# Threshold attention with Fourier mixing on one core: other work held back for a mixing, and its sums on VectorE cut into three pieces

## The chip, the cores and the metric

The kernel runs on one NeuronCore of one Trainium2 chip. Its time is the device time of one launch, in microseconds. Lower is better.

## The reference

The program computes an attention with a threshold and, on its result, a mixing by Fourier transforms and a two-layer network. All data are float32.

```python
# q, k, v: (8, 8, 576, 64); tau = 0.02; w_ch1: (512, 2048); w_ch2: (2048, 512)
scores = q @ k.T / sqrt(64)
scores = where(scores >= max(scores) - tau, scores, -1e9)
attn   = softmax(scores) @ v                      # (B, H, S, D)
x      = attn.transpose(0, 2, 1, 3).reshape(B, S, H * D)   # (8, 576, 512)
mixed  = real(fft(fft(x, axis=1), axis=2))
u      = x + mixed
un     = (u - mean(u)) / sqrt(var(u) + 1e-6)      # over the last axis
out    = u + maximum(un @ w_ch1, 0) @ w_ch2
```

## The kernel before, in words

**Attention.** There are 8 batches of 8 heads. Two heads make a pair, so a batch has 4 pairs, and a pair has 5 steps of 128 query rows (`NT = 5`, the last one holds what is left of both heads). A batch is thus 20 steps (`per_batch`), and the whole program 160. Step `i` calls `scores(i)` (L424, TensorE into the PSUM tile `sc`), `softmax(i)` (L451: maxima at L462 and threshold at L478 on VectorE, the exponential at L470 on ScalarE, the division at L494 on VectorE), `weights_in_parts(i - 1)` (L511: TensorE transposes of the step before, at L540 and L559, copied to SBUF by ScalarE), and twice per pair `weighted_values` (L568).

**Mixing.** When a pair is complete, `fold_rows` (L610) adds and subtracts its rows against each other, on GpSimd for the first three pairs of a batch and on VectorE for the last (L619), into the tile `f`. Then `mixing(b)` (L660) makes the transform of batch `b`. It is a Python generator, and each `yield` ends one of its steps. Its first step holds all the sums across the chunks of `f` on VectorE: two by `fold_chunks` (L650, L651) and five at L669, L675 and L678. Two empty steps follow. The next six make matmuls `py` from `f` (L689) and copy them to `y_e` and `y_o` on ScalarE (L694, L699). The last five are matmuls `pa` (`over_seq`, L702) whose results go through the tile `tmp` (ScalarE L721, VectorE L725 and L726) and are added to the attention's result on GpSimd (L728, L732), which writes the tile `u_t`. That is 14 steps.

**Groups.** The network works on groups of tokens: one of 384, one of 128 (`channels`, L828), then sixteen of 256 tokens, numbered 2 to 17 (`channels_in_quarters`, L1035). Each of those sixteen multiplies 2x2 blocks with seven products in place of eight. Its first product, `hidden_in_quarters` (L885), is 14 pieces of 16 matmul records (L923) each; VectorE adds their PSUM banks to the tile `hs` (L932), ScalarE copies some and takes the Relu (L937), VectorE and GpSimd form the sums of weights (L906). The three pieces `first`, `others`' sixth and `others`' seventh accumulate in one PSUM bank, `banks["sum"]`: the sixth is read by VectorE (L973) before the seventh is added to the same bank (L982). Its second product is seven products of 4 pieces each (L1064, matmuls at L1066). GpSimd forms sums of `hs` (`s_form`, L1062), VectorE sums of `w2` (`combine`, L1027), and VectorE adds each result to the rows (`Rows.add`, L801); SyncE then issues the store (L808). One bank, `sum_`, is held from its first product to its sixth. All these PSUM tiles share one pool of four banks (tag `mm`) with the mixing's and with the attention's transposes.

**The planner.** TensorE's order is written out by `fill` (L1137), which is called three times in each step. Each call adds `per_slot` to a budget, takes one step of a mixing if there is one, and then takes pieces of group work while less has been spent than the budget. Group work of a batch may start once that batch's mixing is done (`work[0][0] < mixed`). The unit is a matmul's row count times four; a piece of the first product is 4096 units, a piece of the second 2048, a whole group 115712, of which the second product is 57344. A mixing is 19240 units, spread over its last 11 steps. At the end of a batch's last step, `start_batch` (L1260) queues the next mixing and the groups that it completes, and sets `per_slot` so that after 60 calls the work left over is `keep` (L1269). So while a mixing runs, TensorE fills the time with the attention and with what `keep` left of the group before. For all batches but the first, `keep` is 0.4 x 198144 = 79258 units. Batches 1 to 7 bring 2, 2, 3, 2, 2, 2 and 3 groups of 256 tokens. After step 160 there is no attention; `per_slot` is then 4953 units until everything is done. This stretch is called the drain below. In steps 20 to 39 (`second_batch`) the order on all engines is by hand; from step 40 on only TensorE's is, and the other engines' order is chosen by the compiler's scheduler, which takes ready instructions by their place in the program.

Of the kernel before, what the change touches and what calls it, by code (L numbers as in the profile page):

```python
# [12 lines left out]
ALU = mybir.AluOpType  # L13
# [5 lines left out]
def _reversed(ap):  # L19

    n = ap.shape[1]
    return bass.AP(
        tensor=ap.tensor,
        offset=ap.offset + n - 1,
        ap=[list(ap.ap[0]), [-1, n]],
    )
# [21 lines left out]
def kernel(  # L48
# [12 lines left out]
    nc = tc.nc  # L61
    B, H, S, D = q.shape
    DM = H * D
# [13 lines left out]
    GT, BT = 384, 256  # L77
    FIRST = 2
    NG = FIRST + (B * S - GT - 128) // BT
    NK = NJ // 2  # L80
# [12 lines left out]
    f = const.tile([128, ND, 2 * FW], FP32, name="f")  # L93
# [77 lines left out]
    for u in range(2):  # L171
# [10 lines left out]
        out=q_scale[:], in0=tau_t[:], scalar1=0.0, scalar2=SCALE, op0=ALU.is_ge, op1=ALU.mult  # L182
# [3 lines left out]
        out=below[:], in0=tau_t[:], scalar1=0.0, scalar2=-3.0e38, op0=ALU.is_lt, op1=ALU.mult  # L186
# [3 lines left out]
        out=tau_pos[:], in0=tau_t[:], scalar1=0.0, scalar2=-1.0, op0=ALU.max, op1=ALU.mult  # L190
# [79 lines left out]
    plus, minus, flip = (factors[:, c : c + 1] for c in range(3))  # L270
# [378 lines left out]
    def fold_chunks(eng, b, c):  # L649
        eng.tensor_tensor(out=sums[b][:, c, :], in0=f[:, c, :], in1=f[:, c + 2, :], op=ALU.add)  # L650
        eng.tensor_tensor(  # L651
            out=f[:, c + 2, :], in0=f[:, c, :], in1=f[:, c + 2, :], op=ALU.subtract
        )
# [6 lines left out]
    def mixing(b):  # L660
        x = xs.pop(b)
        slot = slice(S * (b % 2), S * (b % 2) + S)

        E, O = slice(0, FW), slice(FW, 2 * FW)
        fold_chunks(nc.vector, b, 0)
        s01 = sums.pop(b)
        nc.vector.tensor_tensor(out=f[:, 0, E], in0=s01[:, 0, E], in1=s01[:, 1, E], op=ALU.add)  # L669
        for out_, in0, factor, in1 in (  # L670
            (f[:, 1, E], s01[:, 1, E], flip, s01[:, 0, E]),
            (f[:, 2, E], f[:, 3, E], minus, f[:, 2, E]),
            (f[:, 3, O], f[:, 2, O], plus, f[:, 3, O]),
        ):
            nc.vector.scalar_tensor_tensor(  # L675
                out=out_, in0=in0, scalar=factor, in1=in1, op0=ALU.mult, op1=ALU.add
            )
        nc.vector.tensor_tensor(out=f[:, 0, O], in0=s01[:, 0, O], in1=s01[:, 1, O], op=ALU.subtract)  # L678
        for _ in range(3):
            yield 0  # L680

        COS = ((0, 0, 65), (1, 65, 129), (2, 129, 257))
        SIN = ((0, 0, 128), (3, 128, 256))
        for u, r, n in ((0, 0, 128), (1, 128, 48), (2, 176, 128)):
            for odd in range(2):
                py = ps.tile([128, 512], FP32, tag="mm", bufs=4, name="py")
                table, first = (dim_s, 0) if odd else (dim_c, 1)
                for c, c0, c1 in SIN if odd else COS:
                    nc.tensor.matmul(  # L689
                        py[0:n, c0:c1], f[:, c, odd * FW + r : odd * FW + r + n],  # L690
                        table[:, c0:c1], start=True, stop=True, skip_group_check=True,
                    )
                y = y_o if odd else y_e
                nc.scalar.copy(  # L694
                    y[0:n, u, 0:256].rearrange("p (g hi lo) -> p lo hi g", hi=2, lo=2),
                    py[0:n, first : first + 256].rearrange("p (lo hi g) -> p lo hi g", lo=2, hi=2),
                )
                if not odd:
                    nc.scalar.copy(y[0:n, u, 256:257], py[0:n, 0:1])  # L699
                yield MIX / 11  # L700

        def over_seq(y, odd, cols, m):  # L702
            pa = ps.tile([128, 512], FP32, tag="mm", bufs=4, name="pa")
            for parity, u, table, extra in ((0, 0, seq_even, seq_xe), (1, 2, seq_odd, seq_xo)):
                at = pa[0:m, parity:KH:2]
                nc.tensor.matmul(  # L706
                    at, y[:, u, cols], table[:, odd, :], start=True, stop=False,
                    skip_group_check=True,
                )
                nc.tensor.matmul(  # L710
                    at, y[:, 1, cols], extra[:, odd, :], start=False, stop=True,
                    skip_group_check=True,
                )
            return pa

        for t in range(2):
            cols = slice(128 * t, 128 * t + 128)
            tmp = sb.tile([128, 3, KH], FP32, tag="tmp", bufs=1, name="tmp")
            low, high, sin = (tmp[:, c, :] for c in range(3))
            pb = over_seq(y_o, 1, cols, 128)  # L720
            nc.scalar.copy(sin, pb[:, 0:KH])  # L721
            yield MIX / 11
            pa = over_seq(y_e, 0, cols, 128)

            nc.vector.tensor_tensor(out=low, in0=pa[:, 0:KH], in1=sin, op=ALU.subtract)  # L725
            nc.vector.tensor_tensor(out=high, in0=pa[:, 0:KH], in1=sin, op=ALU.add)  # L726
            def add(c, rows, first, second, eng=nc.gpsimd):
                eng.tensor_tensor(  # L728
                    out=u_t[rows, c, slot.start : slot.start + KH],
                    in0=x[c][rows, 0:KH], in1=first, op=ALU.add,  # L730
                )
                eng.tensor_tensor(  # L732
                    out=u_t[rows, c, slot.start + KH : slot.stop],
                    in0=x[c][rows, KH:S], in1=_reversed(second[:, 1:HALF]), op=ALU.add,
                )

            every = slice(0, 128)
            add(t, every, low, high, nc.vector if b == 0 and t == 1 else nc.gpsimd)
            add(3 - t, every, high, low)
            if t == 1:  # L740
                add(3, slice(0, 1), high[0:1, :], low[0:1, :])
            yield MIX / 11
            if t == 1:

                pa = over_seq(y_e, 0, slice(256, 257), 1)
                nc.scalar.copy(sin[0:1, :], pa[0:1, 0:KH])
                add(2, slice(0, 1), sin[0:1, :], sin[0:1, :])
                yield MIX / 11
# [4 lines left out]
    def tokens_of(g):  # L753

        if g < FIRST:
            return ((0, GT), (GT, 128))[g]
        return GT + 128 + BT * (g - FIRST), BT

    def cost(g):

        n = tokens_of(g)[1]
        both = NJ * ND * n + NJ * DM * n // 128
        return 4 * (both if g < FIRST else both * 7 // 8) + ND * n
# [64 lines left out]
    def channels(g):  # L828
        rows = Rows(g)
        n = tokens_of(g)[1]  # L830
        h = [hs[:, n * j : n * (j + 1)] for j in range(NJ)]
        for j in range(NJ):
            hidden(g, j, j, h[j])
            yield 4 * ND * n
            if j in (2, 5) and j // 3 < rows.nt:
                rows.load(j // 3)
                yield ND * 128
            if j == 11:
                rows.factors(0, min(rows.nt, 2))
        if g == FIRST - 1:  # L840
            first_sums_w1()
        for t in range(rows.nt):
            po = ps.tile([128, DM], FP32, tag="mm", bufs=4, name="po")
            for j in range(NJ):
                nc.tensor.matmul(  # L845
                    po[:, :], h[j][:, 128 * t : 128 * (t + 1)], w2[j],
                    start=(j == 0), stop=(j == NJ - 1),
                )
                if j % 2 == 1 and j < NJ - 1:
                    yield 2 * 4 * DM  # L850
            rows.add(t, slice(0, DM), po[:, :])
            rows.store(t)
            yield 2 * 4 * DM
            if t + 2 < rows.nt:
                rows.load(t + 2)
                rows.factors(t + 2, t + 3)
                yield ND * 128
# [402 lines left out]
    def start_batch(b):  # L1260

        nonlocal groups, todo, per_slot, budget
        mixes.append(mixing(b))
        todo += MIX
        while groups < NG and sum(tokens_of(groups)) <= (b + 1) * S:
            work.append((b, channels(groups) if groups < FIRST else channels_in_quarters(groups)))
            todo += cost(groups)
            groups += 1
        keep = 0.4 * cost(0) + (cost(1) if b == 0 else 0)  # L1269
        per_slot = (todo - spent - keep) / (3 * per_batch)  # L1270
        budget = spent

# [10 lines left out]
    def second_batch(i):  # L1283
# [10 lines left out]
        if first == 0:  # L1294
# [5 lines left out]
            while folds:  # L1300
                fold_more()
            load_v(n + 1)
            start_batch(0)
            mix(3)
            mix(3)
# [123 lines left out]
```

## Time and profile before

| what | value |
|---|---|
| three runs, us | 1720.28, 1721.44, 1721.71 (median 1721.44) |
| the profiled execution's own time, us | 1722.82 |
| its span, first to last instruction, us | 1721.0 |
| mean granted TensorE clock | 0.987 |
| TensorE matmul busy, us (share) | 1639.9 (95%) |
| VectorE busy, us (share) | 1187.5 (69%) |
| ScalarE busy, us (share) | 776.9 (45%) |
| GpSimd busy, us (share) | 655.1 (38%) |
| VectorE sums of the last mixing start, us | 1518.05 |

The page gives busy time, engine by engine, then the span cut into 40 slices, then the chain of work that ended last, and then groups of equal instructions. A group's line ends with the idle time its engine had just before them and with what ended it. A line of a timeline gives start, duration, engine, source line and the tiles written and read; a figure in square brackets is how long the engine had stood idle before, and the instruction after the arrow ended that wait. Two matmul records belong to one float32 matmul, and their durations overlap, so durations of a run of them are read from the merged line of the timeline and not from the mean of one. Steps, calls and leftover work are not in the profile; they follow from the planner's arithmetic above.

### The profile page before, as it was taken

What the parts mean: (1) busy time and instruction counts of PE and PEld (TensorE: products, weight loads), DVE (VectorE), ACT (ScalarE), POOL (GpSimd) and SP (SyncE); (2) the same over time, 40 slices, a digit from 0 to 9 for tenths busy, and PEclk for the clock granted to TensorE, in tenths of its full rate; (3) what the DMA queues carried; (4) which work ended last, traced back from release to release, by engine and by line L of the source; (5) the groups of instructions that cost most, each with busy time, mean ns of one, the idle gap of its engine ahead of it and who ended that gap; (6) DMA issues with size and microseconds to landing.
All of it is one profiled execution on the core that took longest, in us unless ns stands there. A gap on an engine that the chain in (4) does not pass through costs nothing.

```text
span 1721.0 us, 28994 instructions
## 1 busy us (share of the span) xinstructions
PE 1639.9 (95%) x10838; PEld 1288.7 (75%) x10838; DVE 1187.5 (69%) x2710; ACT 776.9 (45%) x1735; POOL 655.1 (38%) x827
## 2 busy tenths in 40 slices
PE   8988899999998999999999899989999899989998
PEld 4555555467787787878788778777878688889998
DVE  6885786657666777767677777777687767754555
ACT  5864675433545353535354435354545435332111
POOL 5773563041422533243451154215250344235333
PEclk9999999999999999999999999999999999999999
DMA  5323222010010001001010000101111010000000
GB/s 160 110 53 106 71 71 54 14 34 21 20 36 17 17 23 41 22 15 34 13 29 27 22 24 12 41 22 22 27 28 34 15 34 1 14 1 13 13 13 13
DMA packets 130385, 57.49 MB, mean 33 GB/s; under 512 B 121123, under 2 KB 121125, under 8 KB 130246
## 3 DMA queue, kind: packets, MB, share of 16 engines
q1 hardware_dynamic: 128854, 55.35, 11.9%
q8 instruction: 86, 1.41, 0.4%
q14 instruction: 53, 0.43, 0.1%
q10 hardware_dynamic: 1392, 0.30, 0.1%
HBM read 46.02 MB, written 9.44 MB: 32 GB/s over the span
## 4 chain that ended last, share of the span: by engine, by line
PE 77%; DVE 12%; ACT 7%; issue 2%; POOL 1%; DMA 1%; SPq 0%; DVEq 0%; ACTq 0%; POOLq 0%
PE po L1066 22%; PE ph L923 21%; PE pv L588 8%; PE sc L434 7%; PE pw L559 5%; PE po L845 3%; DVE e L478 2%; ACT e L470 2%; DVE neg L462 2%; PE sc L445 2%; PE ph L819 1%; PE py L689 1%; PE pa L706 1%; PE pd L112 1%; PE pa L710 1%
## 5 line engine op out<-in xcount | busy, mean ns | idle before, releaser
L462 DVE TENSOR_REDUCE neg<-sc 128x1 f32<-128x576 f32 x288 | 205.7, 750 | 184.2 <-PE sc L434 170.8
L470 ACT ACTIVATE e<-sc,neg 128x576 f32<-128x576 f32 x288 | 211.8, 735 | 245.4 <-DVE neg L462 244.8
L478 DVE SCALAR_TENSOR_TENSOR e<-sc,thr,e 128x576 f32<-128x576 f32 x288 | 226.9, 813 | 52.5 <-ACT thr L474 52.0
L1066 PE MATMUL po<-w,hs 128*128 128x256 f32 x1024 | 243.2, 383 | 0.2
L923 PE MATMUL ph<-u_t,w 128*128 128x128 f32 x1536 | 196.6, 284 | 28.1 <-DVE hs L932 24.4
L923 PEld LDWEIGHTS ph<-u_t,w 128*128 128x128 f32 x1536 | 186.1, 199 | 34.2 <-DVE hs L932 25.9
L1066 PEld LDWEIGHTS po<-w,hs 128*128 128x128 f32 x1024 | 186.5, 190 | 33.3 <-issue 10.8
L561 ACT COPY e_t<-pw 128x512 f32<-128x512 f32 x256 | 148.5, 594 | 88.9 <-PE pw L559 88.7
L559 PE MATMUL pw<-ident,e 128*128 128x128 f32 x1152 | 170.2, 274 | 11.4 <-ACT kT L407 2.9
L434 PE MATMUL sc<-kT,qT 64*128 64x288 f32 x1024 | 168.0, 433 | 7.8 <-DVE e L478 7.1
L932 DVE TENSOR_TENSOR hs<-ph,hs 128x512 f32<-128x512 f32 x160 | 107.2, 684 | 78.0 <-PE ph L923 60.0
L559 PEld LDWEIGHTS pw<-ident,e 128*128 128x128 f32 x1152 | 134.5, 141 | 32.0 <-issue 4.7
L434 PEld LDWEIGHTS sc<-kT,qT 64*128 64x128 f32 x1024 | 92.7, 188 | 69.4 <-issue 42.5
L801 DVE SCALAR_TENSOR_TENSOR u<-po,rstd,u 128x256 f32<-128x256 f32 (+1 forms) x164 | 75.8, 482 | 85.4 <-PE po L1066 82.5
L937 ACT ACTIVATE hs<-hs 128x512 f32<-128x512 f32 x128 | 79.8, 631 | 118.7 <-DVE hs L932 118.6
L494 DVE TENSOR_SCALAR e<-e,den 128x576 f32<-128x576 f32 x216 | 129.3, 635 | 2.8
L923 PE MATMUL ph<-t_u,s_w 128*128 128x128 f32 x1024 | 125.2, 276 | 1.1 <-ACT y_e L699 1.0
L1062 POOL TENSOR_TENSOR s_tile<-hs 128x512 f32<-128x512 f32 x32 | 45.6, 1425 | 209.3 <-ACT hs L937 154.7
L923 PEld LDWEIGHTS ph<-t_u,s_w 128*128 128x128 f32 x1024 | 119.0, 192 | 5.1 <-issue 1.9
L1066 PE MATMUL po<-hs,s_tile 128*128 128x256 f32 x512 | 121.3, 381 | 0.0
L1066 PEld LDWEIGHTS po<-hs,s_tile 128*128 128x128 f32 x512 | 93.7, 190 | 13.7 <-issue 2.6
L906 POOL TENSOR_TENSOR s_w<-w,w 128x512 f32<-128x512 f32 x32 | 40.1, 1274 | 161.9 <-PE ph L923 161.9
(195 smaller groups left out, 2914.5 us busy)
## 6 DMA issues: line engine op xcount, KB each, us to landing
hs<-in_moe_w_ch_dram SPq DMA_DIRECT2D x23, 512.0 KB, 4.3
out_dram<-u SPq DMA_DIRECT2D x36, 256.0 KB, 2.0
qk_in<-in_q_dram SPq DMA_DIRECT2D x64, 128.0 KB, 2.4
v_in<-in_v_dram SPq DMA_DIRECT2D x64, 128.0 KB, 2.5
qk_in<-in_k_dram SPq DMA_DIRECT2D x31, 128.0 KB, 2.4
w<-in_moe_w_ch_dram SPq DMA_DIRECT2D x6, 512.0 KB, 8.2
qk_in<-in_k_dram SPq DMA_DIRECT2D x31, 64.0 KB, 2.3
stage<-in_moe_w_ch_dram SPq DMA_DIRECT2D x3, 512.0 KB, 3.9
```

What stands on the lines that cost most here:

```text
L434: nc.tensor.matmul(sc[j][:, c, 0:HALF], qT[hp, 128 * t : 128 * t + 128], kT[hp, HALF * c : HALF * (c + 1)], start=True, stop=True,)
L462: nc.vector.tensor_reduce(out=neg[:, j : j + 1], in_=sc[j][:, :, 0:HALF], axis=AXIS_XY, op=ALU.max, negate=True,)
L470: nc.scalar.activation(out=ej, in_=sc[j][:, :, 0:HALF], func=ACT.Exp, bias=neg[:, j : j + 1], scale=1.0)
L478: nc.vector.scalar_tensor_tensor(out=ej, in0=sc[j][:, :, 0:HALF], scalar=thr[:, j : j + 1], in1=ej, op0=ALU.is_ge, op1=ALU.mult, accum_out ...
L494: nc.vector.tensor_scalar(out=e[:, S * j : S * (j + 1)], in0=e[:, S * j : S * (j + 1)], scalar1=den[:, j : j + 1], scalar2=None, op0=ALU.mult,
L559: nc.tensor.transpose(pw[:, c, :], e[:, c0 : c0 + 128], ident[:, :])
L561: nc.scalar.copy(e_t[:, 4 * j : 4 * j + 4, qs], pw[:, :, :])
L588: nc.tensor.matmul(pv[64 * j : 64 * j + 64, 0:m], vt[:, 2 * c + j, :], e_t[:, 4 * j + c, 0:m] if c < 4 else ends[:, 0:m], start=(c == 0), ...
L923: nc.tensor.matmul(banks[name][:, 128 * q : 128 * q + 128], left[c][:, 512 * part + 128 * q : 512 * part + 128 * q + 128], right[c], start ...
L932: nc.vector.tensor_tensor(out=to, in0=bank, in1=to if other is None else other, op=ALU.add)
L937: nc.scalar.activation(out=to, in_=to, func=ACT.Relu)
L1066: nc.tensor.matmul(bank[:, 0 : DM // 2], left[p], right[p], start=start and p == 0, stop=p == NK - 1, skip_group_check=True,)
```

## The change

Two edits. The first cuts the mixing's first step: the two `fold_chunks` sums stay in it, the next two sums (those of chunks 0 and 1, even part) move to the second step, and the last three (chunk 2 even, chunk 3 odd, chunk 0 odd) to the third. The number of steps stays 14, and the seven instructions, their operands and their order among themselves stay too. The second edit sets `keep` to 57344 units for all batches but the first, which is exactly the second product of one group of 256 tokens; the first batch's stays `0.4 * cost(0) + cost(1)`, since the conditional expression takes in the whole sum.

```diff
         E, O = slice(0, FW), slice(FW, 2 * FW)
         fold_chunks(nc.vector, b, 0)
+        yield 0
         s01 = sums.pop(b)
-        nc.vector.tensor_tensor(out=f[:, 0, E], in0=s01[:, 0, E], in1=s01[:, 1, E], op=ALU.add)
-        for out_, in0, factor, in1 in (
-            (f[:, 1, E], s01[:, 1, E], flip, s01[:, 0, E]),
-            (f[:, 2, E], f[:, 3, E], minus, f[:, 2, E]),
-            (f[:, 3, O], f[:, 2, O], plus, f[:, 3, O]),
-        ):
+
+        def fold(out_, in0, factor, in1):
             nc.vector.scalar_tensor_tensor(
                 out=out_, in0=in0, scalar=factor, in1=in1, op0=ALU.mult, op1=ALU.add
             )
+
+        nc.vector.tensor_tensor(out=f[:, 0, E], in0=s01[:, 0, E], in1=s01[:, 1, E], op=ALU.add)
+        fold(f[:, 1, E], s01[:, 1, E], flip, s01[:, 0, E])
+        yield 0
+        fold(f[:, 2, E], f[:, 3, E], minus, f[:, 2, E])
+        fold(f[:, 3, O], f[:, 2, O], plus, f[:, 3, O])
         nc.vector.tensor_tensor(out=f[:, 0, O], in0=s01[:, 0, O], in1=s01[:, 1, O], op=ALU.subtract)
-        for _ in range(3):
-            yield 0
+        yield 0
...
-        keep = 0.4 * cost(0) + (cost(1) if b == 0 else 0)
+
+        keep = 0.4 * cost(0) + cost(1) if b == 0 else 4 * 7 * NK * DM // 2 * BT // 256
         per_slot = (todo - spent - keep) / (3 * per_batch)
```

## The prediction

> **What bounds the kernel now.** I read the page first: busy time, and the chain that ended last.
>
> ```profile
> PE 1639.9 (95%) x10838; PEld 1288.7 (75%) x10838; DVE 1187.5 (69%) x2710; ACT 776.9 (45%) x1735; POOL 655.1 (38%) x827
> PE 77%; DVE 12%; ACT 7%; issue 2%; POOL 1%; DMA 1%; SPq 0%; DVEq 0%; ACTq 0%; POOLq 0%
> L923 PE MATMUL ph<-u_t,w 128*128 128x128 f32 x1536 | 196.6, 284 | 28.1 <-DVE hs L932 24.4
> ```
>
> TensorE (PE) is the bound: idle only 1721.0 - 1639.9 = 81.1 us. Of that, 24.4 us are one wait: products of `hidden_in_quarters` (L923) for VectorE's add L932. Where they lie, PE's timeline tells, here the two kinds of it:
>
> ```profile
> 722.64 2.05 PE L923 MATMUL ph<-u_t,w 128*128 128x128 f32 x16 [2.40 <-DVE hs L932]
> 960.42 3.47 PE L923 MATMUL ph<-u_t,w 128*128 128x128 f32 x16 [4.88 <-DVE hs L932]
> 968.03 2.05 PE L923 MATMUL ph<-u_t,s_w 128*128 128x128 f32 x16 [1.12 <-ACT y_e L699]
> ```
>
> Each of the mixings 2 to 7 has one: 2.40, 2.40, 4.88, 5.09, 4.83, 4.34, sum 23.94 us, and none lies elsewhere at this size. Next, VectorE's timeline around the one at 960:
>
> ```profile
> 948.42 0.82 DVE L621 TENSOR_TENSOR half<-x 128x287 f32<-128x287 f32 x2 [2.56 <-issue]
> 951.51 0.77 DVE L650 TENSOR_TENSOR sums<-f 128x608 f32<-128x608 f32 x1
> 952.21 0.68 DVE L932 TENSOR_TENSOR hs<-ph,hs 128x512 f32<-128x512 f32 x1
> 955.05 1.07 DVE L669 TENSOR_TENSOR f<-sums 128x304 f32<-128x304 f32 x1
> 956.11 1.47 DVE L675 SCALAR_TENSOR_TENSOR f<-sums,factors 128x304 f32<-128x304 f32 x1
> ...
> 959.31 0.46 DVE L678 TENSOR_TENSOR f<-sums 128x304 f32<-128x304 f32 x1
> 959.69 0.68 DVE L932 TENSOR_TENSOR hs<-ph,hs 128x512 f32<-128x512 f32 x1
> ```
>
> VectorE works without a gap from 948.4 to 961.6: last pair's folding, softmax, the seven sums. The second L932 reads the sixth product; PE needs that bank for the seventh. It runs only after all seven sums, at 959.69, and PE stands from 955.5 to 960.4. Last, the stretches after the stalls (columns: window, length, busy of PE, PEld, DVE, ACT, POOL, granted clock, DMA):
>
> ```profile
> 960.00:964.00 4.00, 3.58 (x18) 3.46 (x20) 1.57 (x4) 0.00 (x0) 0.00 (x0) 0.57 0.00 0
> 1147.00:1154.00 7.00, 4.08 (x18) 3.85 (x20) 4.26 (x11) 0.00 (x0) 0.00 (x0) 0.55 0.00 0
> 1339.00:1346.00 7.00, 6.19 (x26) 4.94 (x27) 3.40 (x7) 1.23 (x2) 0.00 (x0) 0.52 0.00 0
> 1523.00:1530.00 7.00, 4.98 (x23) 4.98 (x24) 3.65 (x8) 0.00 (x0) 0.00 (x0) 0.51 0.00 0
> ```
>
> The clock is near half: 16 records take 3.47 to 3.78 us against 2.05. Each long stall is paid twice.
>
> **What the Trainium skill says.** "TensorE: Matmul & The Clock Gate", Part 1, says the array's clock falls to half after an idle window of about 3.4 us and returns after a busy one. The trace agrees: half clock follows the stalls of 4.3 to 5.1 us, one of the two of 2.40 us (0.78 at 535 to 539), not the other. The same page (Architectural detail) calls VectorE a strict first-in, first-out queue; so an add behind a sum waits for it, as at 959.69. "SBUF — State Buffer", Who interferes with whom, says a VectorE instruction with two SBUF inputs and a GpSimd one that reads SBUF lock each other out. The trace fits: L669 takes 0.47 us with GpSimd idle and 1.07 beside its L1062.
>
> **Edit two: work left over.** By the planner's sums, today's 79258 units are the 57344 of a second product and 21914 of the first: 5.35 pieces. They fill the mixing's first calls, so the sixth and seventh products fall exactly on VectorE's seven sums. With 57344 all L923 work lies before the mixing, and L1066 work fills it. Removed from the collision:
> - the six stalls: 23.9 us.
> - the slow clock after them: PE busy x (1 - clock), 3.58 x 0.43 + 4.08 x 0.45 + 6.19 x 0.48 + 4.98 x 0.49 = 8.8, and 1.2 at 531 to 539 (1.60 x 0.21 + 4.00 x 0.22): 10.0 us.
> - waits of L923 on banks in the same stretches, for L699 1.02 to 1.12 (four) and for L547 1.21 and 1.20: 6.6 us.
>
> Together 40.5 us. Mixing 3 is my model for the new order: it has two or three group pieces per call and already runs its `py` and `pa` beside L1066; there, after its stall, PE never waits as long as 0.4 us. The two held banks (`sum_` and one `po`) thus leave enough.
>
> Moved: 21914 units go from the drain into the calls of batch 1; later batches hand on equal amounts. At 1.95 us per 4096 units that is 10.4 us of PE work, and the drain shrinks by it. I cost it at nothing, because PE is the bound in both (191.18 of 196.0 us busy in 329 to 525); without that cover it would be worth up to -10.4. Moved with the second product past the mixing's steps: L1062 on GpSimd (4 x 2 of about 1.3 us), 16 `combine` of 0.6 and 10 adds of 0.48 on VectorE, two stores on SyncE's queue. The pieces of L923 that leave take 4 or 5 L932 and up to 4 L906 with them, so VectorE's load in the mixing (38.0 of 49 us in 951 to 1000) stays about equal. GpSimd is idle there until its sums (10.9 us before 954.5). The stores come earlier by some pieces, ahead of loads that are issued a pair in advance: nothing.
>
> What is lost is cover **behind** a mixing. Two-group batches keep 12288 units (5.4 us of PE, beside the attention) after its last step; enough for GpSimd's adds to `u_t`. Mixing 3 and the drain keep none:
> - In the drain, the last `pa` end at 1551.24, GpSimd's last add to `u_t` at 1559.04, 7.8 us later. Before, PE had L1066 work until 1564.5. Now it has one product, 3.6 us, then wants `u_t`. Wait 4.2 us at most by this trace; 1.3 less, since a L1062 (1.26) at 1549.86 will have run earlier. I take 2.5 us, plus 1.5 for a possible slow clock; from 0 to 7.8 + 3.4.
> - In mixing 3 calls 13 and 14 have no group work, and the first new products need chunks 0 and 1: `u_t` ready at 764.5, t1 at 765.7, PE there at about 764 to 766. I take 0.7; from 0 to 3.
>
> **Edit one: the sums in pieces.** Same seven instructions, about 5 to 6 us. Nothing runs less. After it, the third piece is issued two calls later, next to the first `py`, which PE meets in the fourth call. `py` stands in PE's queue, and behind it that step's L1066 pieces and transposes, so all of PE waits if it is late. For mixing 4: PE without the stall does scores (1.2), seven L1066 pieces (6.3), transposes (1.3) and scores (1.2) from 947.8, and meets `py` at 957.9. VectorE: folding to 950.2, maxima to 951.5, piece one to 953.1, L478 twice to 955.1, piece two 1.0 to 2.5 to about 957, L494 to 958.2, the chunk-2 sum of piece three to 958.7. Wait 0.8 to 1.2; I take 0.9 in six mixings, 5.4 us. From 0 (scheduler keeps the sums together) to the rival below. Steps 20 to 39 issue all three pieces at once: nothing.
>
> Left over: a third of the small bank waits (6.6) stays, 2.2. **Sum:** -40.5 + 5.4 + 4.0 + 0.7 + 2.2 = -28.2 us. Against the profiled execution's own 1722.82 (span 1721.0 and 1.8 around it) that is 1694.6; the median of the runs lies 1.4 lower, so 1693.2, rounded 1693. The small y_e wait of mixing 1 (2.53 at 323.9) is behind other work and stays.
>
> **Rivals.**
> - *Half the hole comes back.* VectorE is the chain in 948 to 960 in any case, and PE only meets it elsewhere: at `py`, or at transposes of the step before. For it: no VectorE gap there. Against it: two L932 and two L906, 2.6 us, leave that stretch. With 3 us per mixing instead of 0.9, six times 2.1 = 12.6 more, and slow clock at three of them, 4 us: 1710.
> - *Slower: the third piece falls behind the next softmax.* If the scheduler puts the next step's maxima and L478 (with its wait for ScalarE, some 4.3 us) ahead of piece three, `py` waits for both: about 7 us in each of six mixings, and 2.5 of slow clock. 57 in place of 5.4: +23 us, 1745. It decides from (40.5 - 6.9) / 6 = 5.6 us per mixing, slow clock included. Against it: the pieces come before that softmax in the program.
> - *No change.* The stalls are only moved, at about the same size: 1720 to 1722.
>
> **Chances.** This measurement can tell about 0.2%, 3.4 us, from no change. The forecast, 1680 to 1702: 0.58. Half returns, 1702 to 1718: 0.22. Over 41 us gained: 0.02. Within 0.2%: 0.06. Slower: 0.12. So faster 0.82. The forecast's own range takes in the drain's 0 to 11, `py`'s 0 to 1.5 six times and the move's -10.4; the range given, 1680 to 1718, adds the second case and leaves 0.2 out.
>
> **What would show it.** Right: no L932 wait of PE over 1 us at the six mixings, clock 1.0 after them, L1066 beside L650 to L678, the drain's start later and shorter by about 10. Wrong: PE waits at L689 for L675 or L678, over 3 us; PE idle before the first L923 of mixing 3 or the drain over 5; or stalls of the softmax in L434. A faster time with those L932 waits still there would refute the cause.

## The result, and the profile after it

| kernel | median, us | runs from - to, us | ratio to the kernel before [95%] |
|---|---|---|---|
| before, beside it | 1721.03 | 1720.28 - 1721.71 | |
| changed | 1728.29 | 1726.82 - 1731.76 | 1.0045 [1.0028, 1.0063] |

The forecast was 1693 us, with a range up to 1718. The changed kernel is 7 us slower. The prediction was wrong in sign.

First the page of the changed kernel: busy time, the chain, and the group of the products that stood in the six stalls. From L689 on, lines have moved by 2: L923 is now L925, L932 is L934, L1062 is L1064, L1066 is L1068. The mixing's sums L669, L675 and L678 are L676, L672 and L681.

```profile
PE 1643.4 (95%) x10838; PEld 1283.3 (74%) x10838; DVE 1198.8 (69%) x2710; ACT 783.0 (45%) x1737; POOL 647.6 (37%) x827
PE 72%; DVE 12%; ACT 7%; POOL 4%; issue 2%; DMA 1%; SPq 1%; ACTq 0%; DVEq 0%; POOLq 0%
L925 PE MATMUL ph<-u_t,w 128*128 128x128 f32 x1536 | 187.5, 276 | 0.6 <-DVE hs L934 0.4
```

The last line says that the predicted removal took place: idle time before this group went from 28.1 to 0.6 us, and its wait for VectorE's add from 24.4 to 0.4. Yet TensorE's (PE's) idle time is 1727.8 - 1643.4 = 84.4 us against 81.1 before. So as much came back elsewhere. The chain names a suspect: GpSimd (POOL) has 4% of it, 1% before.

PE's timeline of the changed kernel shows where. Among the lines with a wait, the first three are of the mixings 2, 3 and 4, and the last three of the steps 112, 132 and 152:

```profile
536.82 0.66 PE L559 MATMUL pw<-ident,e 128*128 128x128 f32 x4 [2.74 <-ACT y_e L701]
728.49 0.71 PE L691 MATMUL py<-dim_s,f 128*128 128x128 f32 x4 [2.76 <-ACT ends L547]
963.90 0.66 PE L559 MATMUL pw<-ident,e 128*128 128x128 f32 x4 [1.16 <-ACT y_e L701]
...
1065.21 3.78 PE L1068 MATMUL po<-hs 128*128 128x256 f32 x8 [4.61 <-POOL hs L1064]
1260.97 3.78 PE L1068 MATMUL po<-hs 128*128 128x256 f32 x8 [4.62 <-POOL hs L1064]
1458.01 3.78 PE L1068 MATMUL po<-hs 128*128 128x256 f32 x8 [4.61 <-POOL hs L1064]
```

Three new stalls of equal size begin some 110 us after the start of the mixings 4, 5 and 6, in a place at which the prediction did not look. Each is a product of a group's second half that waits for a sum of `hs` on GpSimd (`s_form`, L1064). The eight records after it take 3.78 us; the same piece takes 1.89 where there is no wait. "TensorE: Matmul & The Clock Gate" of the Trainium skill, Part 1, puts the fall to half clock at an idle window of about 3.4 us; the three waits of 4.6 us with doubled records agree with that. Shorter waits of this kernel do not, as the last section shows.

GpSimd's timeline around the first of them, after:

```profile
1052.49 0.46 POOL L899 TENSOR_TENSOR t_u<-u_t 128x128 f32<-128x128 f32 x1 [5.38 <-PE ph L925]
...
1055.53 1.54 POOL L621 TENSOR_TENSOR half<-x 128x287 f32<-128x287 f32 x2
1057.03 1.83 POOL L626 TENSOR_TENSOR f<-half 128x143 f32<-128x143 f32 x4
...
1059.25 1.47 POOL L650 TENSOR_TENSOR sums<-f 128x608 f32<-128x608 f32 x1
1060.68 1.44 POOL L1064 TENSOR_TENSOR s_tile<-hs 128x512 f32<-128x512 f32 x1
1062.08 1.64 POOL L651 TENSOR_TENSOR f<-f 128x608 f32<-128x608 f32 x1
1063.69 1.47 POOL L1064 TENSOR_TENSOR hs<-hs 128x512 f32<-128x512 f32 x1
1065.13 1.47 POOL L1064 TENSOR_TENSOR s_tile<-s_tile,hs 128x512 f32<-128x512 f32 x1
```

GpSimd has no gap from 1052.5 to 1066.6. Four things stand in its one queue: the next group's adds to `t_u`, the folding of the batch's second pair, the sums across chunks for the next mixing that follow it (L650, L651), and the sums of `hs`. `s_form` makes each of these in two halves; the first halves have run at 1042 to 1047, and the lines show the second ones. The Relu that they need (L939) ends at 1055.76, but they start at 1060.68 and 1063.69. PE wants the second at 1060.6 and gets it at 1065.2.

Before, the same instructions lie apart:

```profile
1052.66 1.76 POOL L621 TENSOR_TENSOR half<-x 128x287 f32<-128x287 f32 x2 [5.82 <-DMA x<-swap]
...
1058.37 1.48 POOL L651 TENSOR_TENSOR f<-f 128x608 f32<-128x608 f32 x1
1059.81 1.73 POOL L1062 TENSOR_TENSOR s_tile<-hs 128x512 f32<-128x512 f32 x1
...
1072.75 1.44 POOL L1062 TENSOR_TENSOR s_tile<-hs 128x512 f32<-128x512 f32 x1 [0.63 <-ACT hs L937]
1074.27 1.26 POOL L1062 TENSOR_TENSOR hs<-hs 128x512 f32<-128x512 f32 x1
1075.49 1.27 POOL L1062 TENSOR_TENSOR s_tile<-s_tile,hs 128x512 f32<-128x512 f32 x1
```

The folding and its sums are over at 1059.9. The first halves of the group's sums follow at once, the second halves come 13 us later, and PE does not wait for GpSimd there. The folding's place is tied to the attention's steps, the place of the sums of `hs` to the planner. A batch of two groups and a mixing is 250664 units in 60 calls, 4178 per call; 21914 units less left over means that every later piece comes 21914 / 4178 = 5.2 calls, nearly two steps, earlier against the attention. Replayed, the planner's arithmetic starts the second product of groups 9, 11 and 13 in step 111, 131 and 151, and in step 113, 133 and 153 before. The batches 4, 5 and 6 bring two groups each and have the same order of work, so one collision is met three times.

One period, from mixing 5 to mixing 6, by stretches. The start of a step is its first `scores` record; length and PE's busy time (us) are from the windows view. The last two columns are experiments told below.

| steps | before | changed | first edit alone | changed, second pair not folded |
|---|---|---|---|---|
| 121 to 123 (mixing) | 26.61, busy 20.49 | 21.93, busy 18.71 | 20.67, busy 18.71 | 21.93, busy 18.71 |
| 123 to 132 | 82.33, 80.80 | 82.32, 80.42 | 82.33, 80.80 | 83.34, 80.42 |
| 132 to 133 | 10.02, 10.02 | 17.06, 12.44 | 10.02, 10.02 | 9.85, 9.85 |
| 133 to 141 | 71.19, 71.11 | 73.85, 72.75 | 71.20, 71.12 | 73.85, 72.74 |
| sum | 190.2 | 195.2 | 184.2 | 189.0 |

The windows for the first and third row (columns as in the prediction's fence), first of the kernel before, then of the changed one:

```profile
1137.05:1163.66 26.61, 20.49 (x153) 18.03 (x151) 19.54 (x44) 11.48 (x24) 3.88 (x3) 0.87 0.05 12
...
1245.99:1256.01 10.02, 10.02 (x87) 8.46 (x86) 9.46 (x17) 5.92 (x11) 8.47 (x9) 1.00 0.01 2
```

```profile
1146.22:1168.15 21.93, 18.71 (x113) 13.60 (x111) 20.46 (x48) 7.95 (x18) 5.35 (x4) 1.00 0.06 14
...
1250.47:1267.53 17.06, 12.44 (x62) 8.78 (x61) 13.45 (x23) 3.89 (x8) 11.73 (x15) 0.80 0.01 1
```

At the mixing the change brings 26.61 - 21.93 = 4.7 us. The forecast's terms for the six mixings are 40.5 - 5.4 - 2.2 = 32.9, that is 5.5 for each. The gain is lost again in step 132 (+7.0, with the clock at 0.80 and GpSimd busy 11.73 of 17.06 us), and 2.7 more are lost after step 133.

### The profile page after: what moved, and what is told of

It reads as the page before. It is cut to its first block, busy times and chain, and to the rows that moved or that the text cites. A ratio compares the mean times of both kernels' runs of the same rounds, so it can differ in the third digit from the quotient of the medians.

```text
span 1727.8 us, 28991 instructions
## 1 busy us (share of the span) xinstructions
PE 1643.4 (95%) x10838; PEld 1283.3 (74%) x10838; DVE 1198.8 (69%) x2710; ACT 783.0 (45%) x1737; POOL 647.6 (37%) x827
## 4 chain that ended last, share of the span: by engine, by line
PE 72%; DVE 12%; ACT 7%; POOL 4%; issue 2%; DMA 1%; SPq 1%; ACTq 0%; DVEq 0%; POOLq 0%
PE ph L925 22%; PE po L1068 18%; PE pv L588 9%; PE sc L434 6%; PE pw L559 5%; PE po L847 3%; ACT e L470 2%; DVE neg L462 2%; DVE e L478 2%; PE sc L445 2%; PE ph L821 1%; PE py L691 1%; PE pa L708 1%; DVE hs L1029 1%; PE pa L712 1%
## 5 line engine op out<-in xcount | busy, mean ns | idle before, releaser
L462 DVE TENSOR_REDUCE neg<-sc 128x1 f32<-128x576 f32 x288 | 205.9, 751 | 200.2 <-PE sc L434 188.1
L1068 PE MATMUL po<-w,hs 128*128 128x256 f32 x1024 | 248.1, 385 | 2.3 <-DVE u L803 2.0
L1068 PEld LDWEIGHTS po<-w,hs 128*128 128x128 f32 x1024 | 186.7, 191 | 35.7 <-issue 11.3
L925 PE MATMUL ph<-u_t,w 128*128 128x128 f32 x1536 | 187.5, 276 | 0.6 <-DVE hs L934 0.4
L925 PEld LDWEIGHTS ph<-u_t,w 128*128 128x128 f32 x1536 | 178.7, 192 | 5.5 <-issue 1.9
L934 DVE TENSOR_TENSOR hs<-ph,hs 128x512 f32<-128x512 f32 x160 | 106.8, 685 | 75.4 <-PE ph L925 52.4
L494 DVE TENSOR_SCALAR e<-e,den 128x576 f32<-128x576 f32 x216 | 136.6, 669 | 2.5
L925 PE MATMUL ph<-t_u,s_w 128*128 128x128 f32 x1024 | 126.4, 277 | 3.2 <-ACT ends L547 1.3
L925 PEld LDWEIGHTS ph<-t_u,s_w 128*128 128x128 f32 x1024 | 119.3, 192 | 7.3 <-issue 2.3
L1068 PE MATMUL po<-hs,s_tile 128*128 128x256 f32 x512 | 122.9, 384 | 0.0
L939 ACT ACTIVATE hs<-hs 128x512 f32<-128x512 f32 x128 | 79.1, 630 | 86.8 <-DVE hs L934 86.6
L1064 POOL TENSOR_TENSOR s_tile<-hs 128x512 f32<-128x512 f32 x32 | 41.8, 1308 | 168.7 <-ACT hs L939 163.0
L1068 PEld LDWEIGHTS po<-hs,s_tile 128*128 128x128 f32 x512 | 94.0, 191 | 13.8 <-issue 2.1
L1064 POOL TENSOR_TENSOR hs<-hs,s_tile 128x512 f32<-128x512 f32 x32 | 47.2, 1476 | 133.3 <-PE po L1068 127.7
```

The costliest lines, as they stand in the source:

```text
L462: nc.vector.tensor_reduce(out=neg[:, j : j + 1], in_=sc[j][:, :, 0:HALF], axis=AXIS_XY, op=ALU.max, negate=True,)
L494: nc.vector.tensor_scalar(out=e[:, S * j : S * (j + 1)], in0=e[:, S * j : S * (j + 1)], scalar1=den[:, j : j + 1], scalar2=None, op0=ALU.mult,
L925: nc.tensor.matmul(banks[name][:, 128 * q : 128 * q + 128], left[c][:, 512 * part + 128 * q : 512 * part + 128 * q + 128], right[c], start ...
L934: nc.vector.tensor_tensor(out=to, in0=bank, in1=to if other is None else other, op=ALU.add)
L1064: nc.gpsimd.tensor_tensor(out=place[0], in0=place[1], in1=place[2], op=op)
L1068: nc.tensor.matmul(bank[:, 0 : DM // 2], left[p], right[p], start=start and p == 0, stop=p == NK - 1, skip_group_check=True,)
```

## Experiments

"Changed" is the changed kernel, the base of each edit unless another is named.

**1 and 2. Each edit by itself.** The first takes the cut of the sums and leaves `keep` as before; the second takes `keep` and leaves the sums in one piece.

```diff
 # split_alone: the three pieces of the sums, and
-        keep = 0.4 * cost(0) + cost(1) if b == 0 else 4 * 7 * NK * DM // 2 * BT // 256
+        keep = 0.4 * cost(0) + (cost(1) if b == 0 else 0)
 # keep_alone: the changed line of keep in the kernel before, whose sums stay whole
```

> Only the first edit: the mixing's sums in three pieces, the work left over as before (79258 units). Theory A (the loss comes from the shift of the groups against the attention's steps, which edit two makes): no wait of TensorE on GpSimd's L1064 in batches 4 to 6; the six waits on L932's add get shorter, since that add no longer has all seven sums ahead of it; 1695 to 1712 us. Theory B (the pieces themselves cost as much as they save, because the matmuls from f or the copies of y wait): about 1715 to 1730 us, with new waits at the mixings.

> Only the second edit: 57344 units left over, all seven sums in the first step as before. Theory A: the three waits of 4.6 us on L1064 at about 1065, 1261 and 1458 are there, each with its slow clock, and the time is that of the changed kernel within 6 us: 1722 to 1734. Theory B: no such loss without the pieces: under 1712 us.

Measured: the cut of the sums alone takes 1695.82 us, 0.9851 [0.9832, 0.987] of the kernel before (1720.95); the new `keep` alone takes 1732.70, 1.0063 [1.0046, 1.008]. The kernel with `keep` alone has the same three stalls:

```profile
1068.08 3.78 PE L1066 MATMUL po<-hs 128*128 128x256 f32 x8 [4.63 <-POOL hs L1062]
1265.25 3.44 PE L1066 MATMUL po<-hs 128*128 128x256 f32 x8 [4.63 <-POOL hs L1062]
1461.02 3.78 PE L1066 MATMUL po<-hs 128*128 128x256 f32 x8 [4.65 <-POOL hs L1062]
```

So the loss comes with `keep`, and a gain like the one forecast for `keep` comes with the other edit, which the prediction counted as a cost. How it comes about is seen in VectorE's timeline of the first edit alone, at mixing 4:

```profile
947.59 0.68 DVE L934 TENSOR_TENSOR hs<-ph,hs 128x512 f32<-128x512 f32 x1
...
951.38 0.46 DVE L676 TENSOR_TENSOR f<-sums 128x304 f32<-128x304 f32 x1
951.77 0.52 DVE L672 SCALAR_TENSOR_TENSOR f<-sums,factors 128x304 f32<-128x304 f32 x1
952.21 0.97 DVE L672 SCALAR_TENSOR_TENSOR f<-f,factors 128x304 f32<-128x304 f32 x2
953.11 0.46 DVE L681 TENSOR_TENSOR f<-sums 128x304 f32<-128x304 f32 x1
953.49 1.28 DVE L934 TENSOR_TENSOR hs<-ph,hs 128x512 f32<-128x512 f32 x2
```

L934 now gets in ahead of the last five sums, at 947.59, and the next two run right behind these. PE's longest wait there is 1.09 us against 4.88 before, with the same amount of group work left for the mixing. The two steps of the mixings 4, 5 and 6 become 5.2, 5.9 and 6.5 us shorter, and the stretch from step 159 to the end, which holds mixing 7, 5.4. At the mixings 2 and 3 the old waits of 2.40 us have gone too, but others of like size stand in their place, and the two steps change by -0.9 and +1.1 us:

```profile
528.39 1.38 PE L691 MATMUL py<-dim_c,f 128*128 128x65 f32 x6 [2.02 <-DVE f L676]
716.30 1.83 PE L925 MATMUL ph<-t_u,s_w 128*128 128x128 f32 x14 [2.58 <-DVE s_w L908]
```

Between the mixings 4 and 6 all other steps keep their lengths to 0.1 us (the table's first and third column, for one period).

**3. GpSimd's sums of the second pair, one pair later.** Is it those two sums (L650, L651) that make the sums of `hs` late?

```diff
-        if n % NPAIR == 1 and b != 1:
+        if n % NPAIR == (2 if b else 1) and b != 1:
             fold_halves(b)
```

> The changed kernel, with GpSimd's two sums of chunks 1 and 3 (3 us, L650 and L651) issued after the third pair of a batch in place of the second, from batch 2 on. Theory A: the three waits on L1064 go or shrink to under 1.5 us, 7.6 us each: 1703 to 1710 us. Theory C (GpSimd is full there, and the wait only moves by a pair or to the next group): 1718 to 1728 us with a wait of like size elsewhere.

Measured: 1729.46 us, 1.0047 [1.0032, 1.0062], stalls of 4.64, 4.63 and 4.63. But GpSimd's order is the old one in the trace: L650 at 1060.54, L1064 at 1061.97, L651 at 1063.38. The two sums run where they ran, though they stand a pair later in the program; the scheduler takes ready instructions. So this run does not answer the question.

**4. The same sums on VectorE.**

```diff
-        fold_chunks(nc.gpsimd, b, 1)
+        fold_chunks(nc.vector, b, 1)
```

> The changed kernel, with those two sums (chunks 1 and 3) on VectorE in place of GpSimd, at the same place in the program. Theory A: the waits on L1064 shrink by the 3 us that leave GpSimd, with the slow clock behind them: 1705 to 1715 us. Theory C: VectorE, which has 1.6 us more in the same stretch, makes TensorE wait instead: 1718 us or more.

Measured: 1739.45 us, 1.0103 [1.0086, 1.012]. The stalls at L1068 are gone, and three longer ones have come in the same steps, of the transposes for ScalarE's copy. VectorE's timeline there:

```profile
1068.66 1.85 DVE L650 TENSOR_TENSOR sums<-f 128x608 f32<-128x608 f32 x1 [4.11 <-POOL f L635]
1070.54 1.73 DVE L651 TENSOR_TENSOR f<-f 128x608 f32<-128x608 f32 x1
1072.19 1.41 DVE L462 TENSOR_REDUCE neg<-sc 128x1 f32<-128x576 f32 x2
```

VectorE stands 4.11 us at the first sum, which waits for GpSimd's folding (L635), and the next softmax's maxima stand behind it. Then PE waits 5.15 us (before 1074.77, 1272.03 and 1469.89). So the two sums are themselves held up by the folding ahead of them, and VectorE's queue, which now has them, is held up in its turn.

**5. The folding of the second pair left out.** From batch 2 on, the instructions of `fold_rows` for the second pair are skipped; the sums L650 and L651 stay.

```diff
+        if n % NPAIR == 1 and b >= 2:
+            yield
+            yield
+            fold_halves(b)
+            return
```

> The changed kernel without the eight GpSimd instructions that fold a batch's second pair (L621 to L637, about 3.7 us in each batch), from batch 2 on; its transforms then use old rows for that pair, so the output differs. The two sums of L650 and L651 stay. Theory A (GpSimd's queue holds the folding of that pair ahead of L1064 just when a group's second product starts): the waits of 4.6 us on L1064 near 1065, 1261 and 1458 fall under 1 us and their slow clock goes; three times 7.6 us less, 1702 to 1710. Theory D (the sum of hs is late for its own inputs, from VectorE or ScalarE, whatever stands ahead of it): the waits stay above 3 us, 1720 to 1728.

Measured: 1708.57 us, 0.992 [0.9902, 0.9937] of 1721.36. The stalls at L1068 are gone (here L1073, as lines from L618 on stand 5 further down). GpSimd's timeline at the place of the first:

```profile
1055.94 1.41 POOL L904 TENSOR_TENSOR t_u<-u_t,t_u 128x128 f32<-128x128 f32 x3
1057.61 1.26 POOL L1069 TENSOR_TENSOR s_tile<-hs 128x512 f32<-128x512 f32 x1 [0.26 <-ACT hs L944]
1058.95 1.28 POOL L1069 TENSOR_TENSOR hs<-hs 128x512 f32<-128x512 f32 x1
```

The sums start as soon as the Relu is done, and PE takes the second at 1062.21 with no wait. The gain is 1728.3 - 1708.6 = 19.7 us, 6.6 for each of three. The steps 112, 132 and 152 alone become 7.8, 7.2 and 7.7 us shorter: 4.6 of waiting, the rest PE's busy time at half clock. The nine steps before take back 1.0 each time, with a new wait of 1.33 us in the period of the table. Leaving out the folding also takes away some 4 us of GpSimd work per batch, but from step 40 on PE's next longest wait for GpSimd in the changed kernel is 0.94 us, so that saving has hardly another way to the end. The two sums stay in the program, but they no longer wait for a folding and run some 47 us earlier against the steps (the first of them at 1012.49 in place of 1059.25). So what has left the queue ahead of the sums of `hs` is the folding and its two sums together; which part each has in the 4.6 us is not shown. With that, the cause of the three stalls is shown: GpSimd's queue at this phase. They are not all, for 1708.6 is still 12.7 us above the first edit alone.

**6, 7 and 8. Other amounts left over.** If it is a matter of phase, the time must go up and down with the amount, and not along one line.

```diff
-        keep = 0.4 * cost(0) + cost(1) if b == 0 else 4 * 7 * NK * DM // 2 * BT // 256
+        keep = 0.4 * cost(0) + cost(1) if b == 0 else 49152    # 65536, 73728
```

> The changed kernel with 49152 units left over in place of 57344: the second product of the group in question then starts two calls earlier in its batch (step 111, first call, in place of step 111, third call). Theory A (a collision of phases): the wait on L1064 changes greatly from the 4.6 us at this small step, to under 2 us if the sums of hs get ahead of the folding; 1703 to 1718. Theory E (less work left over costs by itself): slower than the changed kernel, over 1730.

> The changed kernel with 65536 units left over: the second product starts one call later than in the changed kernel (step 112, first call), its sums of hs some 3 us later, when the folding of the second pair is nearly done. Theory A: the wait on L1064 shrinks to 0 to 2 us, and two pieces of the first product are all that is left in the mixings' first call: 1698 to 1712. Theory E: between the changed kernel and the one with the first edit alone, in proportion to the units left: about 1716.

> The sums in pieces with 73728 units left over, that is four pieces of the first product and the whole second. Theory A: no wait on L1064 (the second product starts in the third call of step 112), and the time lies with those of 65536 units and of 79258 units: 1690 to 1700. Theory E (time grows with less left over): the same range but in order, between 1695.8 and 1696.4, which tells nothing; a time above 1705 speaks for a collision at yet another phase.

| units left | us | ratio [95%] | PE's longest waits from step 40 on |
|---|---|---|---|
| 49152 | 1716.82 | 0.9972 [0.9962, 0.9982] | 4.57 for `u_t` in the drain; `py` 2.02 in four mixings, 2.19 in the last |
| 57344 (changed) | 1728.29 | 1.0045 [1.0028, 1.0063] | 4.61, 4.62, 4.61 for `hs` L1064 |
| 65536 | 1696.35 | 0.9863 [0.9844, 0.9882] | 2.31, 2.47, 2.46 for `y_e` |
| 73728 | 1706.66 | 0.9913 [0.9898, 0.9928] | 4.02, 2.44 for `hs` L934; 2.34, 2.51, 2.51 for `ends` L551 |
| 79258 (first edit alone) | 1695.82 | 0.9851 [0.9832, 0.987] | 2.58 for `s_w` L908; 2.02 for `f` |

All five have the sums in pieces. 57344 is the worst, both neighbours are better, and the stall for `hs` on GpSimd is in none of the others. So the time does not follow the amount along one line, and "just the second product" is not the best of these five: at each amount other waits are the longest. Two lines stand for that. The first is of 49152 units, the second of 73728:

```profile
1556.53 3.78 PE L925 MATMUL ph<-u_t,s_w 128*128 128x128 f32 x16 [4.57 <-POOL u_t L730]
```

```profile
713.81 2.82 PE L925 MATMUL ph<-u_t,w 128*128 128x128 f32 x16 [4.02 <-DVE hs L934]
```

The first is the lost cover in the drain that the prediction priced at 4.0 us. It is real, with its slow clock (3.78 against 2.05), but at this size it stands only at an amount below the one predicted for. The second is the old stall of an L934, back in spite of the cut.

**9 and 10. Who empties the banks.** What remains are short waits at the mixings for `y_e` (L701) or `ends` (L547), both copies from PSUM on ScalarE. Is ScalarE too late (theory F of the expectations), or are two free banks too few, whoever empties them (theory G)? The copy of one column (L701) goes to VectorE, once in the changed kernel and once at 65536 units.

```diff
-                    nc.scalar.copy(y[0:n, u, 256:257], py[0:n, 0:1])
+                    nc.vector.tensor_copy(y[0:n, u, 256:257], py[0:n, 0:1])
```

> The changed kernel, with the copy of y's single column (L701, three of 128 or 48 elements per mixing) on VectorE in place of ScalarE. Theory F (what is still lost at each mixing is a bank of the first matmuls from f, held because this copy stands in ScalarE's queue behind an exponential that waits for VectorE's maximum): the waits of the transposes on it (2.74, 1.16, 1.16, 1.01 us) go, with some slow clock; the waits on L1064 stay; 1718 to 1725. Theory G (four banks are too few there whoever empties them): the waits stay, on another copy; 1726 to 1731.

> 65536 units left over, the sums in pieces, and that copy on VectorE. Theory F: the waits on the copy of y (0.92, 2.31, 2.47, 2.46 us) go, 5 to 10 us less than with ScalarE: 1686 to 1692. Theory G: 1694 to 1700.

Measured: 1729.92 us, 1.0051 [1.0036, 1.0066], and 1701.93 us, 0.9895 [0.9878, 0.9912]. The first is no better than the changed kernel, the second no better than 65536 units without it. In the changed kernel the waits only change their name:

```profile
539.18 0.66 PE L559 MATMUL pw<-ident,e 128*128 128x128 f32 x4 [2.85 <-ACT ends L547]
732.59 0.66 PE L559 MATMUL pw<-ident,e 128*128 128x128 f32 x4 [2.15 <-DVE y_e L701]
966.80 0.66 PE L559 MATMUL pw<-ident,e 128*128 128x128 f32 x4 [1.07 <-DVE y_e L701]
```

2.74, 2.76 and 1.16 have become 2.85, 2.15 and 1.07. So ScalarE's queue alone is not the cause. But the copy has not left the softmax behind. First ScalarE in the changed kernel, then VectorE with the copy moved, both at mixing 4:

```profile
963.06 0.74 ACT L470 ACTIVATE e<-sc,neg 128x576 f32<-128x576 f32 x1 [1.10 <-DVE neg L462]
963.70 0.15 ACT L701 COPY y_e<-py 128x1 f32<-128x1 f32 x1
```

```profile
965.27 1.40 DVE L462 TENSOR_REDUCE neg<-sc 128x1 f32<-128x576 f32 x2
966.60 0.14 DVE L701 COPY y_e<-py 128x1 f32<-128x1 f32 x1
```

On ScalarE the copy runs behind an exponential that waited for VectorE's maxima (L462), on VectorE behind the maxima themselves. A copy that comes late behind them fits both runs, and so do too few free banks. Neither was tried by itself: no kernel here frees a bank, or puts the copy ahead of the maxima.

## Why the prediction was wrong

**The step that failed** is the move of 21914 units, of which the prediction said "I cost it at nothing, because PE is the bound in both". It counted the amount of work moved and not the phase: everything in the batches after it runs 5.2 calls earlier against the attention's steps, and "later batches hand on equal amounts" hides just that. It looked at GpSimd's sums (L1062) only at the mixing, where it called GpSimd idle, and not where the next group's sums would land. The bound it gave, "up to -10.4", had no loss side. What the runs showed in its place: three stalls of PE behind GpSimd's queue, worth 19.7 us (experiment 5), which come with `keep` alone as well (experiment 2). None of the prediction's signs of being wrong came true: they look at the mixings, the drain and the scores, and the loss lies elsewhere.

**The rest of the gap.** Forecast to result are 35 us, so some 15 are left. The starts of the steps, in the traces before and after, tell where they lie:

| stretch | changed - before, us (rounded) | forecast |
|---|---|---|
| steps 112, 132, 152 (the stalls) | +22.2 | 0 |
| from there to the next mixing or the drain | +7.7 | 0 |
| mixings 2 to 6, two steps each: -2.2, +0.9, -3.0, -4.7, -3.1 | -12.1 | -27.4 |
| steps 63 to 81 and 83 to 101 | +4.0 | +0.7 |
| steps 43 to 61 (the moved work) | +3.6 | +10.4 |
| mixing 1, two steps | -3.2 | 0 |
| from step 159 to the end (mixing 7 and drain) | -14.1 | -11.9 |
| steps 0 to 41 | -1.1 | 0 |
| sum | +6.9 | -28.2 |

After the stalls, the largest miss is that the mixings 2 to 6 gained 15.3 us less than forecast. The bank waits that stayed are 8.8 us there, 6.6 more than allowed for, and PE's busy time at half clock at the mixings 3, 4 and 6 is some 6 us by the prediction's own formula (24.83 x 0.06 + 20.30 x 0.08 + 21.07 x 0.14). The 7.7 us behind the stalls were located and not explained; the 2.7 us of steps 133 to 141 are there with the second pair unfolded too. The moved work was cheaper than costed, since PE's idle time in steps 43 to 61 fell from 4.8 to 0.5 us. None of these small parts was taken away by itself, so their causes are not proven.

Then the terms, one by one:

- *Six stalls, 23.9 us:* gone, to 0.4. Right. But the forecast gave them to edit two. Edit one alone leaves 1.7 of them, since it lets L934 in between the sums, with other waits in their place at the mixings 2 and 3. The prediction held that edit one only costs 5.4, because it looked at what the pieces do to `py` and not at what may now overtake them.
- *Slow clock after them, 10.0:* gone at mixing 5 (0.87 to 1.00); half clock comes for 3.4 us after the 2.76 at 728 and at the waits of mixing 4, for 6.8 us at those of mixing 6, and for 6.8 us at each of the three new stalls.
- *Bank waits, 6.6, of which 2.2 stay:* wrong. 2.74, 2.76, 1.16, 1.16 and 1.01 remain, 8.8 us. Mixing 3 as a model failed at the model itself: at 728 it now has the 2.76. The rival of half the hole named this place; but the mixings 2 to 6 together still gain 12.1 us, so this rival alone gives a faster kernel.
- *Edit one's `py`, 0.9 per mixing, 5.4 in all:* right in size. PE waits for the sums 0.30 us at mixing 2, 0.66 at mixing 4, 0.66 and 0.81 at each of mixings 5 and 6, and not at the others: 3.9. The rival that put the third piece behind the next softmax did not occur: at mixing 4 the last sum (L681) starts at 961.11 and the next maxima at 962.28.
- *Cover lost in the drain, 4.0:* too high. The wait is 0.94 with no slow clock; it is 4.57, with the slow clock, at 49152.
- *Mixing 1's `y_e` wait of 2.53, "stays":* wrong. It is gone in the changed kernel and with the first edit alone, and still there (2.53) with `keep` alone.
- *Mixing 3's wait for `t_u`, 0.7:* 0.82 at 769.61. Right.
- *The drain shorter by about 10:* from the last mixing's first sum to the end it went from 202.9 to 188.9 us, 14.0 less. That holds mixing 7's own gain too: with it and the lost cover the forecast is 10.4 + 5.5 - 4.0 = 11.9. Right.

So the sum was near at mixing 5 (4.7 of 5.5), too high at the other mixings, where bank waits and half clock stayed, and it was made over too little of the batch.

The best version here is the first edit alone: 1695.82 us, 25 below the kernel before and 32 below the changed one, level with 65536 units (1696.35). That the forecast of 1693 comes near to this time is chance: its gain was reckoned from the other edit.

## What to carry to other kernels

When leftover work is changed in a program whose engines run in order, everything after it shifts against the part with a fixed beat; follow each queue through one whole period, not only the place that is mended, and multiply what is met by the number of equal periods. Try to cut a long block on an in-order engine before moving other work away from it: here the cut let the urgent instruction through and left the phase alone. And test two edits one by one: here one gained 25 us, the other lost 12, and both together lost 7.

## What was not expected of the hardware

- GpSimd is only 37% busy over the span, and its queue stops PE all the same. "TensorE: Matmul & The Clock Gate" of the Trainium skill (Architectural detail) calls its queues strict first-in, first-out, per core of GpSimd; the trace agrees, since the sums of `hs`, whose Relu ended at 1055.76, started at 1060.68 behind the folding.
- At each of the three stalls of 4.6 us the clock was half for 6.8 us. After the wait of 2.76 us at 728 it was half for 3.4 us, after that of 2.74 at 536 it was not. Half clock also came at the mixings 4 and 6, where no wait is over 1.16 us. The windows (columns as above) show how busy PE was, first in the two windows of the wait of 2.74, then at mixing 4 before and during half clock:

```profile
531.96:535.37 3.41, 1.81 (x11) 1.25 (x9) 3.41 (x9) 0.61 (x1) 0.00 (x0) 1.00 0.00 0
535.37:538.79 3.42, 1.75 (x11) 1.51 (x12) 3.36 (x13) 2.68 (x8) 0.00 (x0) 1.00 0.00 0
...
962.04:965.45 3.41, 1.67 (x11) 1.13 (x11) 3.41 (x8) 2.26 (x6) 0.00 (x0) 1.00 0.00 0
965.45:968.86 3.41, 3.41 (x16) 2.53 (x14) 3.41 (x13) 1.21 (x2) 1.39 (x1) 0.50 0.00 0
```

  At mixing 4 PE had been busy for 1.67 of the 3.41 us before half clock; before the half clock at mixing 3 (from 729.93) it was 1.44, and at mixing 6 (from 1354.57) 2.08. So the page's idle window of about 3.4 us was not needed here, and the measurement decides. The three starts of half clock lie whole multiples of 3.413 us apart (965.45 - 729.93 is 69 times, 1354.57 - 965.45 is 114 times). On this grid the wait of 2.74 us falls into two windows, with PE busy 1.81 and 1.75 us, and the clock stayed full. Busy time in one window does not decide alone, since 2.08 was followed by half clock and 1.75 was not.
- Two sums moved from GpSimd to VectorE were not faster there. In experiment 4 they took 1.85 and 1.73 us, against 1.47 and 1.64 on GpSimd in the changed kernel, while sums of the same shape take VectorE 0.78 and 0.77 at a mixing. GpSimd's own three sums of `hs` ran beside them and took 1.26, 1.69 and 1.80 us, against 1.26 to 1.28 alone. This agrees with what the prediction cited from the Trainium skill ("SBUF — State Buffer", Who interferes with whom) on the two engines locking each other out.
